# A recurrent-attention and mixture-of-experts kernel: the weights of the first two experts loaded by blocks of rows

## The chip, the cores and the metric

The kernel runs on one core of a Trainium2 chip. The metric is the time on the device in microseconds (us), from the start of the program to its end; smaller is better. The time before the change is the median of three runs. One further execution was taken with the hardware profiler on, and everything read from the profile or the trace belongs to that execution.

## The reference, cut to what matters

Gated linear attention over 4 batches, 8 heads, 768 positions and head size 48 gives a matrix x of 3072 tokens by 384. Each token then goes to one of 8 experts, each a two-layer network (384 to 1024 to 384).

```python
for t in range(S):                                   # attention, 768 steps
    state = alpha[:, :, t, :, None] * state + np.einsum('bhd,bhe->bhde', k[:, :, t], v[:, :, t])
    y[:, :, t] = np.einsum('bhd,bhde->bhe', q[:, :, t], state)
...
logits = xn @ en.T / tau                             # x and expert_emb, normalised by rows
expert_idx = np.argmax(logits, axis=1)
...
for e in range(E):                                   # experts, E = 8
    mask = expert_idx == e
    h = np.maximum(x[mask] @ w1[e], 0.0)             # w1[e]: 384 x 1024
    out[mask] = gate_w[mask, None] * (h @ w2[e])     # w2[e]: 1024 x 384
```

All of it is in float32. One expert's w1 and w2 have 1.5 MB each.

## The kernel before, in words

**Two stages.** The first walks over 24 chunks of 128 tokens (NS = 24, index s). Within a chunk the recurrence is turned into matrix products: `decays` transposes the inputs and scans them, `scores` makes products of queries and keys (tile `sc`), `mix_states` and `mix_chunk` make the outputs (tile `pyx`), `rows` turns these back into rows of tokens and adds the router's logits. The chunks are pipelined by hand: in step s the kernel works at chunks s, s-1, s-2 and s-3, and the loop runs three steps past the last chunk. The router works on groups of chunks (`choose`, `place`) and sends each token's row by an indirect DMA of GpSimd to the stretch of its expert in a DRAM buffer (`to_rows`, tensor `xs`, line 311).

**Which expert comes first** is known after chunk 15: `first_expert` picks one with at least 256 tokens among the first 16 chunks. So its first 256 tokens can be handled before the router is done: `fetch_early` (line 175) loads their rows into `xg`, `turn_early` transposes them (tiles `pxe`, `exT`), and `first_layer_early` (line 672) computes their first layer in the gaps of the last steps: for each block f of 128 of the 1024 hidden columns, three matmuls over k (KT = 3 blocks of 128 rows of w1) add up in the PSUM tile `phe`, and ScalarE takes the result to `ehT`. That makes 8 values of f. One comes in step 24, between the scores of chunk 23 and `mix_states`, and one more after its `update` place; two more come in the same places of step 25, and four at the ends of steps 25 and 26. [...]the three matmuls of one f are six records of PE and six weight loads (PEld) in the profile.

**Second stage.** The experts run one after the other (`run`, line 1220, then `run_extra`), the first layer by a scheme with fewer products, for which DVE and GpSimd form sums and differences of weights beforehand (`mix_weights`, `mix_first_weights`), so `w_m` in the profile.

**The weights.** `weights(i)` (line 135) reads the number of the i-th expert into a register of the Sync engine (SP) and issues two DMAs there: all of w1 into `w1_s[i % 3]` (128 partitions x 3 x 1024; in each partition three rows of 4 KB), then all of w2 into `w2_s[i % 3]` (128 partitions x 8 x 384; eight rows of 1.5 KB). The row k * 128 + p of the matrix lies in partition p, block k. Nobody can use a part of such a tile before the whole transfer has landed, for the wait is on the transfer.

**Order of the queue.** SP issues in program order: the loads of the chunks, the early rows (line 181), then `weights(0)` (called at line 724, behind the last load of v), then `weights(1)` (line 808). The latter is held back on purpose: a memset of one column of `w1_s[1]` on GpSimd (line 807), placed behind the masking of chunk 23's scores, is written first, and the DMA must wait for it. After that SP waits for the router's counts to `fetch` the rows of experts 0 and 1 (lines 161 to 174), then `weights(2)`, and so on from the loop at line 1354. The order of instructions on TensorE is written out by hand (`in_turn`, line 196, chains each piece to the one before), so that a matmul which waits for weights holds all the later ones.

Semaphores for DMAs are given out by the framework: the transfers of SP use eight of them in turn, and each waits for the one before on the same semaphore.

Of the kernel before, what the change touches and what calls it, by code (L numbers as in the profile page):

```python
# [27 lines left out]
def kernel(  # L28
# [12 lines left out]
    nc = tc.nc  # L41
# [9 lines left out]
    KT = DM // P  # L51
    FT = F // P
# [76 lines left out]
    NW = 3  # L129
    w1_s = [consts.tile([P, KT, F], FP32, name=f"w1_{i}") for i in range(NW - 1)]  # L130
    w2_s = [consts.tile([P, FT, DM], FP32, name=f"w2_{i}") for i in range(NW - 1)]
    w1_r = w1.rearrange("e (k p) f -> e p k f", p=P)
    w2_r = w2.rearrange("e (k p) d -> e p k d", p=P)

    def weights(i):

        e = nc.values_load(
            turn_i[0:1, i : i + 1], engines=(SP,), min_val=0, max_val=E - 1,
            skip_runtime_bounds_check_because="a sum of two experts, less E from E on",
        )  # L140
        nc.sync.dma_start(
            out=w1_s[i % NW], in_=w1_r[ds(e, 1)].rearrange("e p k f -> (e p) k f")
        )
        nc.sync.dma_start(
            out=w2_s[i % NW], in_=w2_r[ds(e, 1)].rearrange("e p k d -> (e p) k d")
        )

    def first_row(i):
        return nc.values_load(
# [11 lines left out]
    def fetch(i):  # L161

        base = first_row(i)
        for t, n in slots(i):

            has = nc.values_load(
                used_i[0:1, i, t : t + 1], engines=(SP,), min_val=0, max_val=1,
                skip_runtime_bounds_check_because="the result of a compare",
            ) > 0
            ins = nc.sync.dma_start(  # L170
                out=xg_s[i % NXG][0:n, t], in_=xs[ds(base + t * P, n)], cond=has
            )
            tc.add_to_no_dep_group("xs", ins.ins)
# [26 lines left out]
    with ExitStack() as c1:  # L200
# [109 lines left out]
        def to_rows(rows, x):  # L310
            ins = nc.gpsimd.indirect_dma_start(  # L311
                out=xs,
                out_offset=bass.IndirectOffsetOnAxis(ap=rows, axis=0),
                in_=x,
                in_offset=None,
                bounds_check=E * N - 1,
                oob_is_err=False,
            )
            tc.declare_no_dep(ins.ins, group="xs", reason="tokens have a row each")
            tc.add_to_no_dep_group("xs", ins.ins)  # L320
            return ins
# [378 lines left out]
        def placing(s):  # L700

            n = None
            for g in placed_at.get(s, ()):
                r = GROUPS[g][1] - 1
                with in_turn():
                    n = place(g, r in (S0 - 1, NS - 1))
                if r == S0 - 1:
                    lead.append(first_expert(n))
            return n
# [8 lines left out]
        for s in range(NS + 3):  # L718
            if s + 2 <= NS:
                v_last = load(s + 2)  # L720
            if s + 2 == NS:

                with tc.issue_after(v_last.ins):
                    weights(0)
# [58 lines left out]
            if 4 <= s < 4 + NXG * (NC + 1):  # L783
                i, t = divmod(s - 4, NC + 1)
# [6 lines left out]
            if s >= NS:  # L791
                n = placing(s)
# [12 lines left out]
            if s == NS:  # L805
                with tc.issue_after(st[NS - 1]["masked"].ins):
                    nc.gpsimd.memset(w1_s[1][:, 0, 0:1], 0.0)
                weights(1)
# [17 lines left out]
    with ExitStack() as c3:  # L826
# [454 lines left out]
        def run_extra(i):  # L1281
            t = blocks_run(i)
            with turn_of(done_pair):
                more = nc.values_load(  # L1284
                    extra[0:1, i : i + 1], min_val=0, max_val=N // HALF,
                    skip_runtime_bounds_check_because="the half blocks of an expert",
                )
            with tc.If(more > 0):
                half_block(
                    w1_s[i % NW], w2_s[i % NW], xT_s[i % 2][:, :, t * P : t * P + HALF],  # L1290
                    gt_s[i % NG][0:HALF, t : t + 1], sx_s[i % NG][0:HALF, t : t + 1],
                )
# [59 lines left out]
            mix_first_weights(1, nc.vector.tensor_tensor)  # L1352
        for i in range(E):
            if i + 2 < E:
                weights(i + 2)
                to_rows(pads[:, i + 2 : i + 3], blank)
                fetch(i + 2)
            run(i)
            run_extra(i)
# [31 lines left out]
```

## Time and profile before

| | |
|---|---|
| median of 3 runs | 408.04 us (407.83 to 408.78) |
| the profiled execution's own time | 416.09 us |
| its span, first to last instruction | 414.2 us |
| mean granted TensorE clock | 0.988 |
| PE busy | 396.5 us, 96% of the span |
| DVE, POOL, ACT busy | 282.9, 220.8, 195.2 us |
| DMA: weights | 16 transfers of 1536 KB |
| HBM read, written | 49.69 MB, 11.45 MB |

The profile is of one execution. PE is the matmul part of TensorE, PEld its weight loads, DVE VectorE, ACT ScalarE, POOL GpSimd, SP the Sync engine, which here only issues DMAs; SPq, PEq and so on are the sequencers. "out<-in" are tiles by the program's names. "L141" is line 141 of the kernel before. A row of the timeline gives the start and the length in us, and in brackets how long the engine had been idle and whose end released it; "issue" there means that it waited for nothing that the profile shows. In the page's slices the span is cut into 40 equal pieces of 10.35 us, and a digit is the busy share in tenths. The ends of matmuls are modelled.

### The profile page before, as it was taken

What the parts mean: (1) busy time and instruction counts of PE and PEld (TensorE: products, weight loads), DVE (VectorE), ACT (ScalarE), POOL (GpSimd) and SP (SyncE); (2) the same over time, 40 slices, a digit from 0 to 9 for tenths busy, and PEclk for the clock granted to TensorE, in tenths of its full rate; (3) what the DMA queues carried; (4) which work ended last, traced back from release to release, by engine and by line L of the source; (5) the groups of instructions that cost most, each with busy time, mean ns of one, the idle gap of its engine ahead of it and who ended that gap; (6) DMA issues with size and microseconds to landing.
All of it is one profiled execution on the core that took longest, in us unless ns stands there. A gap on an engine that the chain in (4) does not pass through costs nothing. (4 is left out here: it accounts for less than half of the span.)

```text
span 414.2 us, 12556 instructions
## 1 busy us (share of the span) xinstructions
PE 396.5 (96%) x4954; PEld 353.6 (85%) x4954; DVE 282.9 (68%) x638; ACT 195.2 (47%) x481; POOL 220.8 (53%) x284
## 2 busy tenths in 40 slices
PE   6999999999999789999999999999999999999994
PEld 6889989898899567679989989899979979979974
DVE  7878979698989216872696695691594389397530
ACT  4455545455555324463653734823651572662320
POOL 7455677776666336721853834822761581682001
PEclk8999999999999899999999999999999999999998
DMA  9999999999987892695604706505601900101001
GB/s 137 158 165 154 152 193 181 193 174 189 206 180 172 283 359 102 183 350 181 220 18 160 254 18 223 183 19 183 227 19 41 358 9 19 40 2 41 15 16 44
DMA packets 119379, 60.28 MB, mean 146 GB/s; under 512 B 102287, under 2 KB 113816, under 8 KB 119312
## 3 DMA queue, kind: packets, MB, share of 16 engines
q1 hardware_dynamic: 115208, 49.14, 49.6%
q0 software_dynamic: 3728, 10.16, 6.8%
q8 instruction: 46, 0.75, 0.8%
q14 instruction: 21, 0.17, 0.1%
q10 hardware_dynamic: 376, 0.05, 0.1%
HBM read 49.69 MB, written 11.45 MB: 148 GB/s over the span
## 5 line engine op out<-in xcount | busy, mean ns | idle before, releaser
L858 POOL DMA_INDIRECT out_dram<-y,sx x25 | 24.6, 983 | 102.8 <-DVE y L1167 42.3
L988 DVE TENSOR_TENSOR hT<-pq,hT 128x512 f32<-128x512 f32 x63 | 43.4, 691 | 46.4 <-PE pq L1088 41.9
L1088 PE MATMUL pq<-xT_m,w_m 128*128 128x128 f32 x560 | 67.2, 275 | 0.0
L1088 PEld LDWEIGHTS pq<-xT_m,w_m 128*128 128x128 f32 x560 | 64.8, 192 | 0.3 <-issue 0.3
L512 POOL TENSOR_TENSOR qs<-qc,a 128x512 f32<-128x512 f32 x24 | 30.6, 1275 | 33.5 <-DVE a L508 17.6
L1040 POOL TENSOR_TENSOR w_m<-w_m,w 128x512 f32<-128x512 f32 x30 | 43.2, 1447 | 1.4
L971 PE MATMUL pyo<-w,hT 128*128 128x384 f32 x128 | 42.6, 486 | 0.0
L1088 PE MATMUL pq<-xT_m,w 128*128 128x128 f32 x280 | 38.4, 277 | 0.6
L993 ACT ACTIVATE hT<-hT 128x512 f32<-128x512 f32 x35 | 22.1, 631 | 31.2 <-DVE hT L988 31.2
L1088 PEld LDWEIGHTS pq<-xT_m,w 128*128 128x128 f32 x280 | 34.9, 192 | 2.1 <-issue 1.8
L971 PEld LDWEIGHTS pyo<-w,hT 128*128 128x128 f32 x128 | 23.7, 190 | 14.8
L479 DVE TENSOR_TENSOR_SCAN r<-pa,inr 128x511 f32<-128x511 f32 x24 | 29.2, 1217 | 7.0 <-PE pa L194 4.6
L191 PE MATMUL sc<-qs,kr 64*64 64x128 f32 x768 | 29.3, 273 | 4.5 <-issue 4.5
L311 POOL DMA_INDIRECT xs<-x,dest x24 | 24.2, 1009 | 14.4 <-DVE x L655 9.4
L508 DVE TENSOR_TENSOR_SCAN a<-pa,ini 128x512 f32<-128x512 f32 x24 | 29.3, 1222 | 1.1
L1160 PE MATMUL pq<-w_m,hT_m 128*128 128x192 f32 x168 | 28.4, 326 | 0.0
L191 PEld LDWEIGHTS sc<-qs,kr 64*64 64x64 f32 x768 | 22.3, 133 | 7.0 <-issue 6.5
L1160 PEld LDWEIGHTS pq<-w_m,hT_m 128*128 128x128 f32 x168 | 27.5, 190 | 0.0
L191 PE MATMUL pyx<-sm,vt 128*64 128x128 f32 x384 | 26.3, 279 | 0.0
L191 PEld LDWEIGHTS pyx<-sm,vt 128*64 128x64 f32 x384 | 20.5, 136 | 4.1 <-issue 3.4
L1040 POOL TENSOR_TENSOR w_m<-w 128x512 f32<-128x512 f32 x12 | 15.3, 1276 | 15.9 <-PE pq L1088 15.9
L651 ACT COPY lg<-pyx 128x32 f32<-128x32 f32 x24 | 4.4, 185 | 41.0 <-PE px L191 35.1
(229 smaller groups left out, 910.3 us busy)
## 6 DMA issues: line engine op xcount, KB each, us to landing
w<-in_moe_w_dram SPq DMA_DIRECT2D x16, 1536.0 KB
kt<-in_k_dram SPq DMA_DIRECT2D x24, 192.0 KB
qt<-in_q_dram SPq DMA_DIRECT2D x24, 192.0 KB
vt<-in_v_dram SPq DMA_DIRECT2D x24, 192.0 KB
xg<-xs SPq DMA_DIRECT2D x22, 196.5 KB
at<-in_alpha_dram SPq DMA_DIRECT2D x24, 168.0 KB
xg<-xs SPq DMA_DIRECT2D x8, 98.2 KB
at<-in_alpha_dram SPq DMA_DIRECT2D x24, 22.5 KB
```

The costliest lines, as they stand in the source:

```text
L191: last["pe"] = nc.tensor.matmul(*args, **kwargs)
L311: ins = nc.gpsimd.indirect_dma_start(out=xs, out_offset=bass.IndirectOffsetOnAxis(ap=rows, axis=0), in_=x, in_offset=None, bounds_check=E ...
L479: nc.vector.tensor_tensor_scan(r[:, L - 2 :: -1], pa[:, L - 1 : 0 : -1], inr[:, L - 2 :: -1], 1.0, ALU.mult, ALU.add,)
L508: d["a_scan"] = by_dve = nc.vector.tensor_tensor_scan(a, pa, ini, 0.0, ALU.mult, ALU.add)
L512: by_pool = nc.gpsimd.tensor_tensor(qs.rearrange("p n t -> p (n t)"), d["qc"], a, ALU.mult)
L858: ins = nc.gpsimd.indirect_dma_start(out=out, out_offset=bass.IndirectOffsetOnAxis(ap=col, axis=0), in_=y, in_offset=None, bounds_check=N - 1,
L971: pe[:] = [nc.tensor.matmul(py, lhsT=hT[:, f], rhs=w2_t[:, f], start=(f == 0), stop=(f == FT - 1),)]
L988: dve[:] = [call(*args, **kwargs)]
L993: act[:] = [call(*args, **kwargs)]
L1040: by(to, x, y, op)
L1088: pe[:] = [nc.tensor.matmul(to[:, f], lhsT=left[:, f * P : (f + 1) * P], rhs=right, start=start and f == 0, stop=stop, skip_group_check=Tr ...
L1160: pe[:] = [nc.tensor.matmul(to, lhsT=left[:, f], rhs=right[:, f], start=start and f == 0, stop=stop and f == n - 1, skip_group_check=True,)]
```

## The change

`weights` gets a second argument. Without it (experts 0 and 1), w1 is loaded in three transfers, one for each block k of 128 rows (0.5 MB, one row of 4 KB in each partition), and w2 in four, of two blocks each (0.4 MB, two rows of 1.5 KB in each partition). With `whole=True` (experts 2 to 7) there are two transfers, as before. All are issued by SP, w1's blocks first, in rising order. The bytes and where they go are the same. Lines below the function move down by one.

```diff
-    def weights(i):
+    def weights(i, whole=False):
...
-        nc.sync.dma_start(
-            out=w1_s[i % NW], in_=w1_r[ds(e, 1)].rearrange("e p k f -> (e p) k f")
-        )
-        nc.sync.dma_start(
-            out=w2_s[i % NW], in_=w2_r[ds(e, 1)].rearrange("e p k d -> (e p) k d")
-        )
+        for w, w_r, n in ((w1_s[i % NW], w1_r, KT), (w2_s[i % NW], w2_r, FT)):
+            step = n if whole else max(n // 4, 1)
+            for k in range(0, n, step):
+                nc.sync.dma_start(
+                    out=w[:, k : k + step],
+                    in_=w_r[ds(e, 1), :, k : k + step].rearrange("e p k f -> (e p) k f"),
+                )
...
-                weights(i + 2)
+                weights(i + 2, whole=True)
```

In the built program SP has ten issues more, and the instructions of the other engines stand in the same order. The waits differ where weights of experts 0 and 1 are first read: the three matmuls of the first f in `first_layer_early` wait for one block each, and the first sums of weights on DVE and GpSimd wait for the blocks that they read.

## Prediction

> **What bounds the kernel now.** I read the page first: busy shares, slices, then the chain of waits, which here holds only the last five pieces of the end and tells nothing of the place that changes.
>
> ```profile
> PE   6999999999999789999999999999999999999994
> PEclk8999999999999899999999999999999999999998
> ```
>
> TensorE is the bound: 9 tenths or more in nearly every slice. One dent lies inside the kernel, slices 13 and 14 (134.6 to 155 us), where the granted clock falls too. There the first weights arrive. Next, the timeline of PE in that stretch (start, length, engine, line, what; in brackets the idle time before and who ended it):
>
> ```profile
> 137.12 1.05 PE L191 MATMUL sc<-qs,kr 64*64 64x128 f32 x29
> 140.75 0.38 PE L191 MATMUL sc<-qs,kr 64*64 64x128 f32 x2 [2.58 <-issue]
> 141.44 2.90 PE L191 MATMUL phe<-exT,w 128*128 128x256 f32 x6 [0.31 <-DMA w<-in_moe_w_dram]
> 144.26 0.90 PE L191 MATMUL pyx<-qs,dec 64*64 64x128 f32 x16
> 145.10 1.09 PE L191 MATMUL pyx<-sm,vt 128*64 128x128 f32 x16
> 146.12 1.56 PE L191 MATMUL phe<-exT,w 128*128 128x256 f32 x6
> ```
>
> Two waits, not one. The last scores of chunk 23 (sc) stop for 2.58 us although no semaphore is awaited there ("issue"); only then does phe, the first matmul that needs w1, wait 0.31 us for its transfer. And phe then takes 2.90 us where the next one of the same shape takes 1.56. The busy time by stretches (the last three columns: granted PE clock, DMA share, GB/s) says why:
>
> ```profile
> core 0: us, PE busy (x) PEld busy (x) DVE busy (x) ACT busy (x) POOL busy (x), PEclk, DMA share, GB/s
> 132.80:137.90 5.10, 5.10 (x158) 4.69 (x149) 3.73 (x10) 3.92 (x14) 3.43 (x9) 1.00 0.88 297
> 137.90:141.40 3.50, 0.64 (x11) 0.15 (x3) 1.05 (x3) 0.34 (x2) 0.16 (x1) 1.00 1.04 375
> 141.40:144.30 2.90, 2.86 (x10) 1.88 (x10) 0.00 (x0) 0.40 (x1) 0.68 (x2) 0.50 0.58 157
> ```
>
> All engines are idle from 137.9 to 141.4 while the DMA engines are full, and then PE runs at half clock. What held sc? The DMA queues in two stretches (queue, kind: packets, MB, share):
>
> ```profile
> q1 hardware_dynamic: 388, 1.27, 95.7%
> ...
> q1 hardware_dynamic: 231, 0.39, 99.7%
> q8 instruction: 1, 0.02, 5.4%
> ```
>
> From 134.5 to 138.35 only weights move; the 16 KB instruction packet comes at last in 138.35 to 139.5. The trace's packet records place it at 138.40, 0.99 us long. Such packets come every 255 records of PE on average (242 to 273 in the eight before it); this one came after 429. It was due at 134.89 (255 records after the last, of 129.71), when PE had 174 records left; they ran out at 137.92, and PE went on at 140.75, 2.35 us after the packet began. So PE starved of instructions behind the weights. The same records show w1's 4 KB packets on 16 rings, 24 on each, from 132.80 on, w2's behind them: 12 rings land w1 by 138.34, the last four at 139.95, 140.31, 140.33 and 141.30.
>
> Last, SP's timeline and waits:
>
> ```profile
> 131.32 0.38 SPq L141 DMA_DIRECT2D w<-in_moe_w_dram  x1
> 131.88 0.37 SPq L144 DMA_DIRECT2D w<-in_moe_w_dram  x1
> SPq L166 <- DVE pads L414: 17.3, 1, 17.3
> SPq L141 <- POOL w L807: 9.8, 1, 9.8
> ```
>
> An issue costs SP 0.56 us, start to start; after expert 1's weights SP idles 17.3 us.
>
> [...]
>
> **The change part by part.**
>
> (1) Instruction packet. w1 now goes in three transfers of 8 packets per ring. [...]the packet due at 134.89 waits for one block. On its ring in the kernel before, 138.40 was either after 16 packets (0.34 us each from 132.80; the first block ends at 135.6) or after all 24 (0.23 each; the block then in progress ends at 136.6). PE resumes 2.35 later, 137.95 to 138.95: a stall of 0 to 1.0 us in place of 2.83. [...]
>
> (2) First matmul. phe's three steps over k now wait for a block each. The last block still ends when w1 ended: same bytes, same rings, 141.30 at worst; 138.34 if the four late rings lose their lateness. I take 141.30. Two of three steps are then done, and the third remains: 1.56/3 = 0.52 us at full clock, 2.90/3 = 0.97 at half. In between PE stands still, so the clock is open. Full clock: phe ends 141.82, pyx(dec) takes 0.60 (its length at 150.17) to 142.42, against 145.10: 2.7 us gained. Half clock: 142.27, then 0.84 and 1.02 x 0.84/0.60 = 1.43, to 144.54, and the second phe ends 146.2 against 147.68: 1.5 us gained. Mean 2.1.
>
> (3) Does it reach the end? From 145 to 165 the others wait on PE: at_row on pyx (16.3 us), xs on x (9.4), SP's fetch on pads (17.3). After 190 PE is full. Next to be late would be expert 1's weights; their last packet comes at 153.9, the first reader (DVE, L988) starts at 161.94, 8 us later. And the placeholder memset that holds them (L807) follows sc, so it moves forward too. I pass on all of it.
>
> (4) Ten more issues. Five more for expert 0: 5 x 0.56, the last at 134.7; w1's are in by 132.44, before the first w1 packet moves, and w2's first packet is at 137.55, so no ring runs dry. For expert 1: 2.8 us later on SP, covered by the 17.3 us of idleness and the 8 us of (3); without these covers 2.8 us. In the built program a transfer takes one of eight semaphores in turn and waits for the transfer eight before; expert 1's last waits for expert 0's third block of w2, landed by 145.4. Nothing on the path.
>
> (5) Extra waits: two on PE, two on DVE's mixing, one or two per Pool mix. The shortest issue gaps here are 0.17 us; [...]0.1 us; bounds 0 and 0.5.
>
> (6) Bookkeeping of the rings. Nearest row: expert 2's four xg transfers, 201 KB each, land 0.5 us apart: 402 GB/s, no gap. Taken 0; the upper bound is the last rival.
>
> Sum: 416.09 (span 414.2 and 1.9 around it) - 2.1 + 0.1 = 414.1 for an execution under the profiler. The median, 408.04, is 8.05 below; I carry the difference over: 406.0.
>
> **The rivals.**
>
> A, the fetch stays late. [...]sc ends at 141.13 as now, all blocks have landed but the last, and only the 0.31 us goes: 407.7. For it: the packet of 177.48, during expert 2's weights, was also about 1.7 us late and not at the end of a transfer.
>
> B, the late rings recover. If lateness comes from three 4 KB rows 512 KB apart per partition, blocks avoid it: w1 lands near 138.4, phe ends at 139.9, clock full: 144.26 - 139.9 + 0.24 = 4.6 us, 403.4; with half of that recovered, 404.7. For it: w2, with other strides, runs at full rate. Against: nothing says what the lateness is.
>
> C, slower: each transfer pays its own start. Every whole w1 shows it, here expert 2's:
>
> ```profile
> 173.00:174.00 1.00, 1.00 (x8) 0.73 (x7) 1.00 (x2) 0.19 (x1) 0.70 (x1) 1.00 1.05 165
> 174.00:175.00 1.00, 1.00 (x11) 1.00 (x11) 1.00 (x4) 0.28 (x1) 0.98 (x1) 1.00 0.91 198
> 175.00:176.00 1.00, 1.00 (x11) 1.00 (x10) 1.00 (x3) 0.00 (x0) 0.70 (x1) 1.00 0.86 340
> ```
>
> 165, 198 and 340 GB/s (the last column), then 426 in the next slice: (261 + 228 + 86)/426 = 1.35 us lost per transfer. If two more blocks pay it, w1 lands at 144.0, [...]the second phe ends near 149.2 against 147.68: 1.5 us slower, 409.5. It decides from a landing later than about 142.7, half of that loss. Against it: rings run on without a common restart, and xg's four in a row show none.
>
> That the blocks aren't made isn't a rival: side by side, SP has ten more issues and PE's order is the same.
>
> **How the numbers follow.** Likeliest, 406.0 (own range 405.3 to 406.7): 0.46. A: 0.24. B, 403.4 to 404.8: 0.13. C, 408.5 to 409.5: 0.15; the rest 0.02. About 0.2%, 0.8 us, is what a measurement can tell from no change. Faster: likeliest and B, 0.59; same: A, 0.24; slower: C and the rest, 0.17. The range, 403.9 to 408.9, leaves out the best of B and the worst of C.
>
> **What would show it.** Right: the instruction packet near 136, sc without a stall over 1 us, phe's first step before 140 and its last near 141.3, the memset L807 about 2 us earlier, the rest of the span moved as a block. Wrong: a packet still at 138.4 (A); w1 landed by 139 (B); blocks landing after 142.7 (C); or the lead of 2 us at 146 gone by 190, which would mean a wait I took for PE's belongs to something else.

## The result, and the profile after

The changed kernel took 407.36 us (median of 22 runs, 404.58 to 410.42), the kernel before 409.98 in the same comparison (22 runs, 407.83 to 413.24): a ratio of 0.9945, 95% interval 0.9925 to 0.9966, so 2.25 us less by this ratio. (The two medians alone are 2.62 us apart; ratios here are those on record, which are not quotients of the medians.) The forecast had 2.04 us less. Later, on another chip, the same two kernels gave 1.0027 (1.0003 to 1.0051): there the change cost 1.1 us, just clear of no change. Both are results, and what follows has to explain the two.

The record doesn't name the chip of the first comparison. On the second and third chip of the experiments 12 of 115 runs of the kernel before lie in a slower group above 417.7 us, so a ratio there also depends on how many runs of a kernel fall into that group.

The profiled execution of the changed kernel took 406.35 us (span 404.6), that of the kernel before 416.09 (span 414.2). PE's last records are 9.5 us apart, most of which is not the change: matched by the number of PE's records, 2.6 us of them have arisen before the first weight moves, and 3.6 come after 147 us of the kernel before. A second trace of the kernel before (e1 below, span 406.4) is the fairer one, and stands beside the first from here on.

The page of the changed kernel, busy share and granted clock of TensorE by slices:

```profile
PE   7899999999999899999999999999999999999994
PEclk9999999999999999999999999999999999999999
```

The dent of two slices has become one, and the clock doesn't fall (1.00 from 134.9 to 138.7 us). PE's timeline of the changed kernel in that place (start, length, engine, line, what; idle time before and who ended it):

```profile
136.81 0.38 PE L192 MATMUL sc<-qs,kr 64*64 64x128 f32 x2 [1.35 <-issue]
137.12 1.56 PE L192 MATMUL phe<-exT,w 128*128 128x256 f32 x6
138.61 0.67 PE L192 MATMUL pyx<-qs,dec 64*64 64x128 f32 x16
139.21 1.09 PE L192 MATMUL pyx<-sm,vt 128*64 128x128 f32 x16
140.23 1.56 PE L192 MATMUL phe<-exT,w 128*128 128x256 f32 x6
```

The same stretch in the second trace of the kernel before:

```profile
136.56 0.38 PE L191 MATMUL sc<-qs,kr 64*64 64x128 f32 x2 [1.42 <-issue]
138.80 1.53 PE L191 MATMUL phe<-exT,w 128*128 128x256 f32 x6 [1.87 <-DMA w<-in_moe_w_dram]
140.26 0.67 PE L191 MATMUL pyx<-qs,dec 64*64 64x128 f32 x16
140.86 1.09 PE L191 MATMUL pyx<-sm,vt 128*64 128x128 f32 x16
141.89 1.56 PE L191 MATMUL phe<-exT,w 128*128 128x256 f32 x6
```

From the end of the stall of sc to the end of the second phe: 141.79 - 136.81 = 4.98 us after, 143.45 - 136.56 = 6.89 before, so 1.91 us gained, about what the spans differ by (406.4 - 404.6 = 1.8). The stall of sc ahead of it is the same, 1.35 and 1.42. What has gone is the wait of phe for w1, 1.87 us. (In the first trace of before, phe waited only 0.31 us since sc was 2.58 late, and then ran at a granted clock of 0.50, from 141.39 to 144.80 us: 147.68 - 140.75 = 6.93 us for the same stretch.)

Why w1 is there earlier is seen in how the 16 rings start (a ring is the share of a transfer that one of the 16 DMA engines carries). The sign is the DMA share (the column before the last) in the first four microseconds from w1's first packet. First the second trace of the kernel before, then the changed kernel:

```profile
core 0: us, PE busy (x) PEld busy (x) DVE busy (x) ACT busy (x) POOL busy (x), PEclk, DMA share, GB/s
130.25:132.25 2.00, 2.00 (x60) 1.83 (x54) 1.94 (x5) 1.79 (x6) 1.06 (x6) 1.00 0.70 228
132.25:134.25 2.00, 2.00 (x63) 1.77 (x61) 1.28 (x4) 1.23 (x3) 1.75 (x3) 1.00 1.00 334
```

```profile
130.48:132.48 2.00, 2.00 (x60) 1.83 (x54) 1.97 (x4) 1.85 (x7) 1.52 (x6) 1.00 0.95 280
132.48:134.48 2.00, 2.00 (x63) 1.77 (x62) 0.46 (x2) 1.38 (x4) 1.91 (x3) 1.00 1.01 369
```

With e1's whole w1, 30% of the rings' time is idle in the first 2 us: (1 - 0.70) x 16 x 2 = 9.6 us of ring time, against 1.6 with the changed kernel's blocks. The packet records name no ring, but a ring at work shows as a packet under way. One microsecond after w1's first packet, 10 of 16 are at work on w1 in the second trace of before, and 16 in the changed kernel. Following packets that join end to end, in the second trace of before ten rings begin w1 within 0.9 us of the first and six between 1.68 and 2.37 us; in the changed kernel all 16 begin within 0.65. The number of late starters is the number of late landings in the record: six after 137 us there, four in the first trace (starts at 2.01 to 2.22 us, landings at 139.95 to 141.30). The late rings of the prediction are rings that began late. That is not a property of every whole w1: in these two traces of before, the twelve whole w1's of experts 2 to 7 have 13 to 16 rings at work after 1 us, where expert 0's has 12 and 10.

The instruction packet, the other half of the prediction, came in the changed kernel at 134.48, 16 KB and 1.01 us long (here the queues from 134.4 to 135.6 us), due about 132.8:

```profile
q1 hardware_dynamic: 155, 0.42, 95.1%
q8 instruction: 1, 0.02, 5.3%
```

SP issued expert 0's seven transfers from 128.97 us on and expert 1's seven, after the memset that holds them (138.5), from 139.2 to 142.9, with nothing behind them until the rows of 158 us (the view merges the 14):

```profile
128.97 13.92 SPq L144 DMA_DIRECT2D w<-in_moe_w_dram  x14
```

### The profile page after: what moved, and what is told of

Its sections match the earlier page's. It is cut to its first block, busy times and chain, and to the rows that moved or that the text cites. A ratio compares the mean times of both kernels' runs of the same rounds, so it can differ in the third digit from the quotient of the medians.

```text
span 404.6 us, 12589 instructions
## 1 busy us (share of the span) xinstructions
PE 390.8 (97%) x4954; PEld 348.4 (86%) x4954; DVE 281.8 (70%) x638; ACT 195.7 (48%) x481; POOL 218.5 (54%) x284
## 5 line engine op out<-in xcount | busy, mean ns | idle before, releaser
L192 PE MATMUL sc<-qs,kr 64*64 64x128 f32 x768 | 25.9, 271 | 1.3 <-issue 1.3
L192 PEld LDWEIGHTS sc<-qs,kr 64*64 64x64 f32 x768 | 20.9, 133 | 1.9 <-issue 1.8
```

Of the source, the lines that this page charges most:

```text
L192: last["pe"] = nc.tensor.matmul(*args, **kwargs)
```

## The experiments

The runs e1 to e4 were made on one chip, e5 to e8 on a second, e9 to e12 on a third, each in one session; each ratio is against runs of the kernel before on the same chip (medians 407.20, 414.34 and 414.38 us). What the traces show of all, in us; "share" is the DMA share of the first 2 us from w1's first packet, "landed" the time from that packet to w1's last landing, "fetch" the time from it to the instruction packet, "copy" how long ScalarE's second copy of ycols in step 25 began after the products that it copies:

| kernel | expert 0's w1 | share | landed | fetch | sc stall | phe wait | copy | ratio (95%) |
|---|---|---|---|---|---|---|---|---|
| before, first trace | whole | 0.76 | 8.50 | 5.60 | 2.58 | 0.31 | 2.66 | |
| e1, before | whole | 0.70 | 8.42 | 4.12 | 1.42 | 1.87 | 0.05 | 0.9985 (0.9963 to 1.0008) |
| e7 | whole | 0.72 | 6.78 | 5.31 | 1.30 | 0 | 3.49 | 1.0029 (0.9999 to 1.0060) |
| e9, before | whole | 0.59 | 7.07 | 4.60 | 0.47 | 0 | 2.09 | 1.0004 (0.9977 to 1.0032) |
| e11 | whole | 0.64 | 7.25 | 5.31 | 1.04 | 0 | 2.08 | 0.9987 (0.9964 to 1.0011) |
| e12 | whole | 0.86 | 6.17 | 4.08 | 1.02 | 0 | 3.50 | 1.0077 (1.0049 to 1.0105) |
| changed | 3 blocks | 0.95 | 6.91 | 4.00 | 1.35 | 0 | 0.05 | 0.9945 (0.9925 to 0.9966) |
| e3 | 3 blocks | 0.96 | 6.89 | 4.08 | 1.19 | 0.17 | 0.05 | 0.9969 (0.9949 to 0.9989) |
| e4 | 3 blocks | 0.91 | 6.46 | 4.09 | 1.33 | 0 | 0.05 | 0.9967 (0.9944 to 0.9990) |
| e8 | 3 blocks | 0.89 | 6.48 | 5.27 | 1.00 | 0 | 3.51 | 1.0119 (1.0077 to 1.0161) |
| e10, changed | 3 blocks | 0.92 | 5.78 | 4.98 | 0.70 | 0 | 3.48 | 1.0027 (1.0003 to 1.0051) |
| e2 | 2 by partitions | 0.86 | 10.30 | 4.23 | 2.17 | 2.88 | 0.05 | 1.0119 (1.0084 to 1.0153) |
| e5 | 2 by columns | 0.54 | 7.31 | 4.76 | 0.77 | 0 | 2.08 | 0.9998 (0.9975 to 1.0022) |
| e6 | 6 | 0.74 | 8.52 | 4.05 | 0.73 | 0 | 2.78 | 1.0121 (1.0072 to 1.0171) |

**e1, the kernel before again.** No edit.

> The kernel before once more, unchanged, for a second trace of it: 9.5 us lie between the two profiled executions, 2.25 between the medians, so the part of 9.5 us that is chance must be known. All theories: ratio 1.000 (0.998 to 1.002). Theory (the instruction packet held behind w1, then a wait for the whole of w1): the packet of this trace again waits 2.5 to 4 us from its due time, sc stalls for 2 to 3 us with no semaphore awaited, and the first phe takes 2.4 to 2.9 us or waits for w1. Rival (the stall of the first trace was a chance event): a packet that waits under 2 us, no stall over 1.6 us, phe at 1.56.

Measured 0.9985, the packet about 2.6 us late, sc stalled 1.42 us, phe waited 1.87 us and took 1.53 (mean granted clock of the run 0.996). Neither side's signs came in full. The theory's two waits are there again, but in another proportion: the long stall of the first trace was partly chance, and what sc lost less (1.42 in place of 2.58), phe lost more (1.87 in place of 0.31), since w1 landed about as late after its first packet (8.42 and 8.50).

**e2, w1 in two halves of the partitions.**

```diff
-        nc.sync.dma_start(out=w1_s[i % NW], in_=w1_r[ds(e, 1)].rearrange("e p k f -> (e p) k f"))
+        for p0 in (0, HALF) if i == 0 else (0,):
+            p1 = p0 + HALF if i == 0 else P
+            nc.sync.dma_start(out=w1_s[i % NW][p0:p1],
+                in_=w1_r[ds(e, 1), p0:p1].rearrange("e p k f -> (e p) k f"))
```

> Expert 0's w1 in two transfers of 64 partitions each; every matmul still needs both, so no part can be used early, and each transfer still reads a partition's three rows one after the other; all else as before. Theory (shorter transfers let the instruction packet in sooner): the packet waits 1.5 to 2.5 us in place of 3.5, sc stalls 1.0 to 2.0 us, ratio 0.996 to 0.998. Rival 1 (only the finer waits count): stall 2.8, phe waits as before, ratio 0.999 to 1.001. Rival 2 (the order of w1's rows makes the late rings): late rings stay, w1's last landing 7.5 us or more after its first packet, and ratio 0.998 to 1.000 whatever the packet does.

All theories missed: 1.0119, 4.8 us slower by the ratio, 3.6 by the medians (410.78 and 407.20). PE's timeline:

```profile
135.76 0.38 PE L194 MATMUL sc<-qs,kr 64*64 64x128 f32 x2 [2.17 <-issue]
139.02 2.90 PE L194 MATMUL phe<-exT,w 128*128 128x256 f32 x6 [2.88 <-issue]
```

w1 landed 10.3 us after its first packet, at 138.93, just ahead of phe (the profile names "issue", but it is this landing that phe needs). The packet records give the reason: from 131 us on a 4 KB packet takes about 320 ns in the two halves (the median of each microsecond up to 137 is 298 to 331) where the median is 159 in e1's transfer to all 128 partitions. The run still serves as the opposite test: w1 lands later, phe waits longer and takes 2.90 us, as long as at the granted clock of 0.50 in the first trace of before (the mean over this run is 0.984, over e1 0.996), the stretch from sc's stall to the second phe takes 10.09 us in place of e1's 6.89, and the kernel is slower.

**e3, the changed kernel with k backwards.** The first matmul needs the block that lands last, so nothing is used early.

```diff
-                for k in range(KT):
+                for k in reversed(range(KT)):
...
-                        start=(k == 0), stop=(k == KT - 1),
+                        start=(k == KT - 1), stop=(k == 0),
```

> The changed kernel, but the first expert's first matmuls take w1's blocks in the order 2, 1, 0, so that the very first needs the block that lands last: partial landing is not used, transfers and row order are kept. Theory: as the changed kernel to within 0.1% (ratio 0.9945 to 0.996), since there the last block landed 0.3 us after phe began: phe starts 0.3 to 0.5 us later. Rival 1 (the finer waits are the gain): phe waits 1.5 us or more for the last block and the ratio goes to 0.998 to 1.000.

Measured 0.9969, a little above the 0.9945 to 0.996 that the theory had. phe waits 0.17 us:

```profile
134.93 0.38 PE L192 MATMUL sc<-qs,kr 64*64 64x128 f32 x2 [1.19 <-issue]
135.47 1.53 PE L192 MATMUL phe<-exT,w 128*128 128x256 f32 x6 [0.17 <-DMA w<-in_moe_w_dram]
```

So the finer waits aren't the gain: even the last block is there 0.17 us after phe is ready.

**e4, only expert 0's w1 in blocks** (its w2, and all of expert 1, whole).

```diff
+            step = 1 if n == KT and not whole else n
...
+                weights(1, whole=True)
```

> Only expert 0's w1 goes in three blocks; its w2 and all of expert 1 stay whole. Theory (all of the gain lies at the instruction packet and the first reading of w1): 0.994 to 0.997, the packet waits about 1.7 us, phe takes 1.56, block landings as in the changed kernel. Rival 3 (blocks of w2 or of expert 1 matter): half of the gain or less, 0.997 to 0.999, with a difference at 145 us or later in the trace.

Measured 0.9967; PE as in the changed kernel:

```profile
135.88 0.38 PE L192 MATMUL sc<-qs,kr 64*64 64x128 f32 x2 [1.33 <-issue]
136.19 1.56 PE L192 MATMUL phe<-exT,w 128*128 128x256 f32 x6
```

On this chip three blocks of one matrix do in the trace what all fourteen transfers do. (The timed intervals of e1, e3 and e4 touch; it is the traces that separate them.)

**e5, w1 in two halves of the columns**: as many packets per transfer as the whole w1 has, of half the size.

```diff
+        for c0 in (0, F // 2) if i == 0 else (0,):
+            c1 = c0 + F // 2 if i == 0 else F
+            nc.sync.dma_start(out=w1_s[i % NW][:, :, c0:c1],
+                in_=w1_r[ds(e, 1), :, :, c0:c1].rearrange("e p k f -> (e p) k f"))
```

> The kernel before with expert 0's w1 in two transfers by columns: each has all 128 partitions and all three rows of each, in rows of 2 KB: 384 packets per transfer, as the whole w1 has, but half its bytes. New theory (the gain is the start of the rings: of a transfer of n packets the last rings start late in proportion to n, about 2.1 us after the first for 384, 1.1 for 192, 0.7 for 128): four to six rings start w1 about 2 us late, w1 lands 7.5 us or more after its first packet, first phe waits or is slow as before, ratio 0.998 to 1.003. Rival 1 (the bytes of a transfer decide): lag about 1 us, w1 lands by 6.5 us, ratio 0.996 to 0.998. Rival 2 (the prediction's, that the instruction packet gets in earlier with a smaller transfer): packet 2 to 3 us after w1's first in place of 4.1, sc stall under 1 us.

The rings start worst of all here, share 0.54, so it isn't the bytes of a transfer that decide; in that the theory holds. But phe didn't wait: w1 landed 7.31 us after its first packet, at 139.03, and phe was due at 139.15. In this trace w1's first packet is further ahead of PE (4.7 us before the first product pyx<-sel,ycols, 3.2 in e1), and time stays as it was, 0.9998.

**e6, w1 in six blocks** (three of rows, two of columns), expert 1 whole.

```diff
+            for c0 in (0, F // 2) if n == KT and not whole else (0,):
+                c1 = c0 + F // 2 if n == KT and not whole else w.shape[2]
...
+                        out=w[:, k : k + step, c0:c1],
```

> The changed kernel with expert 0's w1 in six blocks (three of rows by two of columns, rows of 2 KB, 128 packets each) and expert 1 whole. Ring start theory: all 16 rings start within 0.8 us, w1 lands within 6.5 us. On the instruction packet: if it waits for a number of packets on its ring ([...]4.1 us), rows of half the size let it in 1.5 to 2 us sooner, the sc stall goes from 1.3 to 0 to 0.6 us and the ratio to 0.991 to 0.994. If it is bytes or time that it waits for, packet at 4.1 us again, stall 1.2 to 1.5, ratio 0.994 to 0.997.

The instruction packet came after 4.05 us. That is no sooner than with blocks on the first chip (4.00 to 4.09), but sooner than in e8 on the same chip (5.27), so whether half-sized rows let it in sooner stays open. All rings began early, within about 0.5 us by the packet records, but ran dry again (share 0.74), and w1 landed after 8.52 us, not 6.5: the smaller rows were no help to the landing. phe didn't wait since it needs the first three blocks only, which were there at 139.01. The time shows nothing: 1.0121 is of six runs, two at 412.61 and 413.86 us, just below the kernel before's median, and four between 419.15 and 419.76, where runs of the kernel before lie too (up to 419.45). The trace is of the first.

**e7, all blocks but w1's of expert 0.**

```diff
-            step = n if whole else max(n // 4, 1)
+            step = n if whole or (i == 0 and n == KT) else max(n // 4, 1)
```

> The changed kernel with only expert 0's w1 whole again; its w2 and expert 1's weights in blocks, so the complement of the run with w1 alone in blocks. Ring start theory: the gain is gone, four to six rings start w1 late, ratio 0.998 to 1.002. Rival (the other blocks carry part of the gain): 0.995 to 0.998, and a lead that arises after 145 us.

There is no gain (1.0029), and the rings start late (0.72). But phe didn't wait for w1, so in this trace there was nothing to gain, and the trace loses time somewhere else, after 148 us.

**e8, all eight experts in blocks** (`weights(i + 2)` without `whole=True`).

> All eight experts in seven transfers each. Five more issues per expert on SP, 2.8 us each time, and rings that start together. Theory: expert 2 and later are prefetched a whole stage ahead and nothing waits for their landing, so the same as the changed kernel, 0.993 to 0.997. Rival (SP's queue is tight later: the fetch of the next rows comes behind the longer list of issues): slower than the changed kernel by 0.2% or more, with a wait for xg or w in the expert loop that the changed kernel doesn't have.

1.0119, slower: all six runs (415.48 to 420.37 us) lie above the kernel before's median. SP's fetch of rows comes at 164.7 us (158.0 in the changed kernel's first trace, 161.5 in e9). It isn't SP's list of issues that delays it: SP is done at 145.2 and waits for the counts, and no weights of experts 2 to 7 have been issued by then. So the rival's sign is right and its cause wrong. What the blocks of these six experts cost by themselves isn't shown: the changed kernel was not run on this chip, and expert 1's blocks alone cost 0.5 to 0.8% on the third chip (e12).

**e9 and e10, before and changed side by side on the third chip.** No edits.

> The kernel before once more, for a trace beside those of the three runs sent with it. Theory (what w1 costs depends on how far its first packet is ahead of PE: 3.2 to 3.7 us ahead of the pxe-following products in the traces where phe waited, 4.7 us where it didn't): with a lead under 4 us the first phe waits 1.5 us or more, or runs at half clock; with 4.5 us or more it waits under 0.3 us. Four to six rings start w1 1.5 to 2.4 us after the first. Ratio 0.998 to 1.002.

> The changed kernel once more, beside a trace of the kernel before from the same chip. Theory: all rings start within about 0.8 us, w1 lands 5.3 to 6.4 us after its first packet, no wait of phe; the sc stall is 1.0 to 1.5 us, about as before, since the instruction packet comes about 4.1 us after w1's first packet in both. Ratio 0.993 to 0.997 where the kernel before waits for w1, and 0.998 to 1.003 where it doesn't. Rival (an earlier instruction packet is half of the gain): packet at least 1 us earlier after w1's first one than in the kernel before, sc stall at least 1 us shorter.

First e9, then e10: the first 2 us of w1, and PE.

```profile
131.88:133.88 2.00, 2.00 (x74) 1.83 (x77) 1.97 (x4) 0.77 (x5) 1.07 (x3) 1.00 0.59 192
```

```profile
138.75 0.38 PE L191 MATMUL sc<-qs,kr 64*64 64x128 f32 x2 [0.47 <-issue]
139.09 1.53 PE L191 MATMUL phe<-exT,w 128*128 128x256 f32 x6
```

```profile
131.65:133.65 2.00, 2.00 (x71) 1.79 (x73) 1.97 (x4) 0.62 (x5) 1.24 (x3) 1.00 0.92 286
```

```profile
138.92 0.38 PE L192 MATMUL sc<-qs,kr 64*64 64x128 f32 x2 [0.70 <-issue]
139.22 1.56 PE L192 MATMUL phe<-exT,w 128*128 128x256 f32 x6
```

The blocks help the rings here too (0.92 against 0.59; w1 landed after 5.78 us, not 7.07), but w1's first packet is 4.7 us ahead of PE's pyx<-sel,ycols products (136.6), not 3.2 as in e1 (133.41 - 130.25), and the whole w1 is down at 138.95, 0.14 us before phe wants it. Nothing to gain, as expected, and the ratio is 1.0027.

**e11, the kernel before with phe moved behind pyx** in step 24, whole transfers: the same matmuls, in another order.

```diff
-            if NS <= s < NS + 2:
+            if s == NS + 1:
...
-                    first_layer_early(2 * (s - NS) + 1, 2 * (s - NS) + 2)
+                    first_layer_early(0 if s == NS else 3, 2 * (s - NS) + 2)
```

> The kernel before, whole transfers, with the first three matmuls groups that need w1 (phe, f = 0 and 1 of the first chunk after the last) moved behind the two products pyx that don't need it: the same matmuls, w1 needed about 1.7 us later. Theory (the first phe's wait for w1 is the whole of the gain): as good as the blocks without any block, 0.994 to 0.997 where the kernel before waits, with the sc stall unchanged. Rival (the blocks gain by the instruction packet or elsewhere): 0.998 to 1.001.

0.9987: no difference, which both sides had for a chip where phe doesn't wait. It settles nothing; it would have had to run on the first chip.

**e12, only expert 1 in blocks** (`weights(0, whole=True)`).

> Only expert 1's weights in seven transfers, expert 0's whole. Theory of the prediction (five more issues at 0.56 us and earlier landings, neither on the path): as before, 0.998 to 1.002. Rival (two of the runs with expert 1 in blocks, the one with all experts and the one without w1 of expert 0, were slower by 0.3 and 1.2% and showed ScalarE held 1.8 us at 152 us by nothing in its queue, and SP's fetch of rows 3 to 5 us late): 1.003 to 1.008, with the same hold of ScalarE.

1.0077, the rival's value: 3.2 us lost by the five transfers that the prediction priced at nothing. The size is less sure than the interval says: 10 of the 22 runs lie above 417.7 us, where the kernel before has 7 of 75; among the others the medians differ by 0.5%, 2.0 us. Where it is lost is seen on ScalarE in step 25 (e9, e10; then e1, where nothing is late):

```profile
149.22 0.37 ACT L623 COPY ycols<-pyx 128x256 f32<-128x256 f32 x1 [2.50 <-PE pyx L191]
150.01 0.37 ACT L623 COPY ycols<-pyx 128x256 f32<-128x256 f32 x1 [0.42 <-PE phe L191]
```

```profile
149.38 0.37 ACT L624 COPY ycols<-pyx 128x256 f32<-128x256 f32 x1 [2.51 <-PE pyx L192]
151.56 0.37 ACT L624 COPY ycols<-pyx 128x256 f32<-128x256 f32 x1 [1.80 <-remote]
```

```profile
147.24 0.81 ACT L623 COPY ycols<-pyx 128x256 f32<-128x256 f32 x2 [0.81 <-PE pyx L191]
```

The products pyx that the second copy waits for end, by the (modelled) records, at 147.91 in e9 and 148.08 in e10. The copy follows 2.09 us later in e9 and 3.48 in e10, and 0.05 in e1. In the four traces with expert 1 in blocks on the second and third chip it is 3.48 to 3.51, in the four with it whole 2.08 to 2.78. PE then stands idle, and in the next phe it runs slower in e12, where the granted clock is 0.50 from 152.5 us for 6.8 us; in e9 it stays at 1.00 there (means over the runs 0.984 and 0.997):

```profile
152.16 2.84 PE L191 MATMUL phe<-exT,w 128*128 128x256 f32 x12
```

```profile
153.60 5.47 PE L192 MATMUL phe<-exT,w 128*128 128x256 f32 x12
```

(e9 and e12.) SP's fetch, which waits for the router's counts, comes later too: 161.46 in e9, 165.98 in e12. On the first chip, expert 1 in blocks made none of this (copy 0.05 in e3, and in the changed kernel). The first trace of the kernel before has it too (2.66). Why ScalarE copies late while expert 1's weights arrive, why not on the first chip, and why blocks make it worse, isn't settled. On the two later chips an instruction packet of PE starts at 150.8 to 151.8 us, which makes a second stall of that kind one candidate, not tested; for e9 it doesn't fit, since the late copy (150.01) began before that packet (151.33).

## Why the prediction was right in number, and where its steps were not

**(1) The instruction packet: wrong.** The step took it that the packet gets in where a transfer ends, which no trace had shown and was the author's assumption, and that the stall of sc would be 0 to 1.0 us. It was 1.35, and 1.42 in e1 without blocks. That PE starves there is borne out: PE goes on 2.2 to 2.4 us after the packet begins in 13 of 14 traces, 2.9 in e2. But the packet started 4.00 us after w1's first packet with blocks, 4.12 in e1 without. Over the traces in the table: whole w1 4.08 to 5.60, mean 4.84; three blocks 4.00 to 5.27, mean 4.48. When it began in the changed kernel, e3 and e4, 17.5 to 18.9 of the 24 packets of w1 on a ring had begun, on the average of the rings: inside the third block. In e4 it was due at 130.7 us, the first block had landed on every ring by 133.08, and it came at 133.53. So the end of a transfer did not let it in; rival A, the late packet, was right on this point, with the chance 0.24. (Counted from when it was due, it was 1.70 us late in the changed kernel, 1.75 in e3 and 2.83 in e4, against 2.5 to 3.5 with a whole w1. So it may have come somewhat sooner in two traces, but the stall was only 0.07 to 0.23 us shorter than e1's.) The stall of 2.83 us that the sum started from was in part an accident of that one execution.

**(2) The first matmul: right size, wrong mechanism.** "The last block still ends when w1 ended ... I take 141.30" is the step that failed. w1 landed 6.91 us after its first packet, not 8.50, with all the rings starting early; the last block was there 0.27 us after phe began, before its third step, and the clock stayed at 1.00. That the late rings recover is rival B, which I gave 0.13; the cause B named, three rows 512 KB apart, isn't shown, since the whole w1's of experts 2 to 7 have the same rows and no such late start. Partial landing, on which my 2.1 us rested, contributed 0.3 us at most (e3 does without it and waits 0.17). That the sum came out is luck, two errors that cancel: a stall of sc that stayed (1.35) and a w1 that came 1.6 us sooner gave 1.91 us in the stretch, where the sum had 2.1.

**(3) Passing it on: right.** 1.91 us at the second phe, 1.8 at the end (e1 against the changed kernel, one trace each).

**(4) Ten more issues at no cost: right for expert 0, wrong for expert 1 on the third chip and, by the traces, on the second.** I looked for a cost in SP's time and in the landing of expert 1's weights. Both covers held; the cost came with ScalarE's late copies at 148 to 152 us, 0.5 to 0.8% in e12. The first trace of the kernel before already shows a late copy, of 2.66 us, and the prediction left out what stands behind slice 14.

**(5)** No cost of the extra waits can be seen: phe begins 0.31 us after the last sc in the changed kernel (136.81 to 137.12), with no wait shown; the 0.1 us in the sum came from no trace. **(6) and rival C:** for expert 0's w1 no start was paid per transfer: the three blocks had all 16 rings at work within 0.65 us (changed kernel), the whole w1 after 2.22 and 2.37 us (the two traces of before). Nor did the rings wait for each other at the end of a transfer: in the first trace of before w2's first packet moved at 137.55, while w1's last ring landed at 141.30. That the clock would stay low for longer, which C's loss of 1.5 us also took, was the author's estimate. The slow start of expert 2's w1 which C would have multiplied is another thing: all 16 rings were at work 0.5 us after its first packet (173.38), but half of the packets of the first microsecond took 0.5 us or more each, in place of 0.16. The smaller size cost nothing in this place: three transfers of 0.5 MB landed in 6.50 us on average (5.78 to 6.91, five traces) and one of 1.5 MB in 7.37 (6.17 to 8.50, six).

Small slips in the working change nothing: 5.60 us over 16 packets is 0.35 each, not 0.34; the second phe of the case of half clock in (2) would end at 146.1, not 146.2; and of the engines called idle from 137.9 to 141.4 DVE was busy for 1.05 us.

The result on another chip, 1.0027, lies just above the range, whose end 408.9 is 1.0021 of 408.04, though its interval reaches into it. My cases had no word for it: that the gain exists only where w1 comes later than phe. Two things decide that. w1's first packet was 3.16 us ahead of PE's pyx<-sel,ycols in e1 and 4.73 in e9, and the whole w1 landed after 8.42 us in e1 and 7.07 in e9; with sc stalled 0.95 us less in e9, a wait of 1.87 us becomes 0.14 us to spare. The lead alone doesn't decide: in e12 it is 3.80, and the whole w1, with 15 of 16 rings at work after 1 us, landed in 6.17 us and phe did not wait. How the two vary from run to run, one trace of each kernel can't show.

What stays open: what limits the start of the rings. For expert 0's w1 the shares follow the packets in a transfer more than the bytes (384 packets: 0.54 to 0.86; 192: 0.86; 128 of 4 KB: 0.89 to 0.96), but the six blocks of 128 packets of 2 KB had 0.74, e12's whole w1 comes close to the blocks, and later whole w1's have no late start, so a count alone isn't the rule. And e12 against e10, 1.0077 and 1.0027, suggests that expert 0's blocks still gain up to half a per cent on the third chip, which the stretch around phe doesn't show (e10 is 0.16 us behind e9 at its end).

## What to carry to other kernels

Judge a large transfer that someone waits for by its last ring: in e1 the whole w1 began 1.68 to 2.37 us late on six of 16 rings, and phe waited 1.87 us for it. Look at the DMA share in its first 2 us, and where it is well below 1 (0.70 in e1), try cutting the transfer along the rows of each partition, which gave 0.95 here and w1 landed after 6.91 us, not along the partitions, which gave 0.86 and 10.30 us (e2). Cut only the one that is waited for: in e12 the same cut on expert 1's weights, which had 8 us to spare in the first trace of before, went with a loss of 2 to 3 us, more than it could ever bring. And a stall seen in one execution is a sample (2.58 us, then 1.42 in e1); before a sum starts from it, a second trace of the same kernel is worth more than any argument.

## What the hardware showed that was not expected

- In two transfers to 64 of 128 partitions each, a packet took twice as long: about 320 ns for 4 KB from 131 us on, in place of 159 (e2).
- With expert 0's whole w1 of 384 packets, four to six of the 16 rings begin 1.7 to 2.4 us after the first (first trace of before, and e1). In e12, and for the whole w1's of experts 2 to 7 in those two traces, 13 to 16 are at work after 1 us.
- TensorE stood still behind weights without waiting for any: its instruction packet, due at 134.9, came at 138.40, and sc stood 2.58 us (first trace of before; 0.47 to 2.58 in all 14 traces).
- Cutting w1 into blocks of rows didn't bring the instruction packet in sooner on the first chip: it began 4.08 and 4.09 us after w1's first packet in e3 and e4, 4.12 in e1.
- The same program differed between chips by 1.8% (medians of the kernel before 407.20 and 414.38 us), and so did the sign of this change (one session on each, so chip and session are not told apart).
